# Where row-half matmuls, token-block outputs and attention heads stand in a fused gated block: a Trainium2 kernel re-ordered

## The chip, the cores and the metric

The kernel runs on one core of one Trainium2 chip. The metric is device time in microseconds (us) of that core. Lower is better. A core has a matrix engine (TensorE, here PE, with its weight loads shown as PEld), VectorE (DVE), ScalarE (ACT), GpSimd (POOL) and SyncE (SP, which here issues most DMAs). Each engine works through its own instructions in order; they wait for each other on semaphores. Matmul results land in PSUM, eight banks of 512 floats in each of 128 partitions; all else is in SBUF.

## The reference

```python
g = _sigmoid((x * gate_w).sum(-1, keepdims=True))         # x: 2048 tokens x 640
a = attention(x, wqkv, w_phi, wo)   # 32 heads of 20; feature maps softmax(pq), softmax(-pq)
b = (_silu(x @ w_gate) * (x @ w_up)) @ w_down             # hidden size 1728
return g * a + (1 - g) * b
# attention: kv = sum over tokens of phi_k x v, z = sum of phi_k
#            o = (phi_q @ kv) / (phi_q . z + 1e-6), then @ wo
```

The attention is linear: all keys and values are summed into one small matrix per head before the first query is used. Inputs and output are bf16.

## The kernel before, in words

There are 16 tiles of 128 tokens and four blocks of four tiles. Everything is issued by one list of short words, `ORDER` (lines 40 to 54); each word calls a small function, and what it emits goes to the end of the queues of the engines it uses. So this list alone fixes the order of work on every engine; a tracker (line 57) adds the semaphore waits that the data needs, by ranges of bytes in SBUF and by whole banks in PSUM. The words used below:

- `K`, `S`, `P`, `E`, `V`: keys, their softmax, and the sum over tokens, up to `N` (line 790). These words, the loads and the first stretch of the list are as before in the changed kernel.
- `Q` t (line 619): the query projection of tile t, ten matmuls of 320 columns, and on ACT two exponentials of it into `eq`, a ring of three buffers. `A`, `B`, `C` t (lines 626 to 648) on DVE: the sums, the product with z, and the scale of that tile; `c` t (line 650): the scaling on POOL into `ph`, and a DMA transpose on SP into `phiT`, which has room for two blocks.
- `O` b.part (line 660): a third of the head outputs of block b, matmuls with 64 columns of weights, two side by side in the two column halves of the array; part 2 also has two of 80 rows by 40 columns. ACT copies the result to `oT` and a small rest to `ol`. `o` b (line 688): four DMAs on SP that put the rest into four rows of each half of `oT`: for each half of the block's columns two, the second of which writes the same byte range as the first and so waits until it has landed.
- `F` b.k (line 697): for block b, hidden chunk k of 128, five matmuls of 512 columns for the gate and five for the up projection; ACT takes a tanh of the gate and a copy of the other, DVE and POOL multiply them into `hT`, which has two buffers (block b uses b modulo 2). The last chunk, k = 13, has only 64 hidden values; it is folded so that two tiles lie in rows 0 to 63 and 64 to 127.
- `W` b.p (line 746): the down projection of that last chunk for two tiles of block b, as row-half matmuls: 64 rows by 128 columns, one tile in the upper and one in the lower half of the array, side by side. It opens the accumulation in two pairs of PSUM banks and holds them. Line 756 interleaves the two tiles' matmuls.
- `D` b.u (line 758): for tile u of block b the other 13 chunks of the down projection and five matmuls per half with `wo`, in all 36 of 320 columns, onto what `W` opened; then ACT scales the sum out of PSUM and SP stores it.

PSUM is handed out as four pairs of banks, the least recently used first (lines 453 to 462), without the held ones. The last tile, 15, uses three column parts (320, 224 and 96 columns) in two pairs, so that its stores can begin early.

`W` is called twice in each block, eight times in all; on PE seven of them stand just ahead of a `D`, and one (`W2.0`) ahead of an `F`. The three `O` parts of a block follow each other on PE, which makes four runs of `O`. `F2` words have six extra ACT waits, on a value long reached, ahead of their tanh (line 723).

Of the kernel before, what the change touches and what calls it, by code (L numbers as in the profile page):

```python
# [1 line left out]

# [1 line left out]

# [4 lines left out]
P = 128  # L9
S_TOK = 2048  # L10
D = 640
# [4 lines left out]
NB = 4  # L16
# [25 lines left out]
U0.3 U1.3 U2.3 U0.4 U1.4 U2.4 V3 Y F0.1 M1 i3 M0 F0.0 M2 V4 M3 M4 K0 K1 I S0 V6 V5 S1 P0 K3 K2 P1 E0  # L42
V9 K4 E1 S3 V7 P3 K5 S2 V8 V10 S4 P2 P4 E2 R0 E3 K6 S5 P5 S6 i4 E4 V14 K7 K8 P6 V15 S7 R2 E5 K9 S8
P7 R1 E6 K10 S9 V12 P8 E7 P9 K11 S10 P10 F0.2 R3 F1.2 E8 E9 K12 E10 S11 S12 K14 S14 V11 K13 P11 P12
E11 K15 P14 R4 S13 P13 F1.9 S15 P15 E12 V13 T F1.8 E13 F1.11 E14 Q1 E15 Q0 Q2 N Z A1 A0 J A2 F0.7
F0.9 F1.4 B0 F1.12 B1 F0.4 L C0 F1.7 c0 F1.10 C1 F0.5 B2 c1 F0.11 Q3 C2 F1.0 F0.8 c2 F0.10 B3 Q4
F1.6 A3 C3 Q5 c3 F1.3 F0.13 F0.12 A4 F0.3 B4 F1.5 F0.6 O0.2 O0.1 O0.0 o0 C4 F1.1 F1.13 B5 A5 C5 Q6
c4 Q7 c5 Q8 W0.0 B7 A6 B6 C6 A7 c6 D0.1 D0.0 Q9 C7 W0.1 B8 A8 D0.2 C8 c7 Q10 D0.3 F2.10 F2.9 F2.2 c8
O1.2 A9 O1.1 B9 O1.0 B10 F2.8 o1 C9 Q11 c9 F2.5 F2.11 F2.4 Q12 B11 F2.3 A10 C10 B12 F2.7 A11 C11
W1.1 D1.3 D1.2 A12 c11 c10 Q14 W1.0 D1.0 A14 C12 D1.1 Q13 F3.2 F3.3 c12 O2.2 O2.1 B13 B14 O2.0 o2  # L50
F2.13 A13 F3.12 F3.5 F2.1 C14 Q15 F3.4 F3.9 F2.12 C13 F2.0 A15 c13 F2.6 c14 B15 F3.1 F3.0 F3.6 C15
c15 F3.13 W2.0 F3.7 D2.1 D2.0 F3.11 O3.2 O3.0 O3.1 F3.8 o3 F3.10 W2.1 D2.3 W3.0 D3.0 D3.1 D2.2 W3.1
D3.2 D3.3
"""


# [143 lines left out]
def _build(nc, A_x, A_wqkv, A_w_phi, A_wo, B_x, B_w_gate, B_w_up, B_w_down, gate_w, out):  # L200
# [5 lines left out]
    def sb(name, shape, dtype):  # L206
        t = nc.alloc_sbuf_tensor(name, list(shape), dtype)
        tr.reg(t, "sbuf", nc.lookup_mloc(t).addr)
        return t
# [9 lines left out]
    ident = sb("ident", [P, P], BF16)  # L219
    us = sb("us", [P, 3, 512], BF16)  # L220
    osb = sb("osb", [P, 4, D], BF16)
    ol = sb("ol", [P, 256], BF16)
    kvsb = sb("kvsb", [P, NCH, 64], BF16)
    hmask = sb("hmask", [P, 3], F32)
    zt = sb("zt", [P, NCH, 3], F32)
# [16 lines left out]
    qd = sb("qd", [P, 2, 32], F32)  # L242
    qc = sb("qc", [P, 2, 66], F32)
    hT = sb("hT", [P, 2, 14, 512], BF16)

    wdbase = nc.lookup_mloc(wd).addr
    v1x = nc.alloc_sbuf_tensor_at("v1x", [P, NT - NV, 33 * 21], BF16, offset=wdbase)
    tr.reg(v1x, "sbuf", wdbase)

    def vbuf(t):  # L250
        return v1r[:, t, :] if t < NV else v1x[:, t - NV, :]
# [28 lines left out]
    def bank(b, c0, c1, r0=0, r1=P):  # L280
        return ps[r0:r1, b * 512 + c0:b * 512 + c1]
# [62 lines left out]
    def memset(e, a, v):  # L344
        eo = tr.eng[e]
        return run(e, lambda: eo.memset(a, v), [], [a])
# [67 lines left out]
    def fills(i):  # L414
        if i < 2:
            v1v = (v1r, v1x)[i][:, :, :].rearrange("p b (h d) -> p b h d", d=DH + 1)
            memset("pool", v1v[:, :, H, :], 0.0)
            memset("pool", v1v[:, :, :, DH:DH + 1], 1.0)
        elif i == 2:
            memset("pool", ekr[:, :, 1280:FK], 0.0)  # L420
            memset("pool", krec[:, :, :], 0.0)
        elif i == 3:
            memset("pool", kvsb[:, :, :], 0.0)
            memset("pool", eq[:, :, 1280:FP], 0.0)
            memset("pool", qc[:, :, :], 0.0)
            memset("pool", hmask[:, :], 1.0)
            select(hmask[:, :], [[-40, 3]], ALU.is_ge, 0.0, 0, 1)
            select(hmask[:, :], [[40, 3]], ALU.is_gt, 0.0, 40, -1)
        else:
            memset("pool", ph[:, :, :], 0.0)  # L430
            memset("pool", zh[:, NCH:P], 0.0)
# [225 lines left out]
           ALU.mult)  # L657
        dma("sp", phiT[:, (t // 4) % 2, t % 4, :, :], ph[:, b, :], transpose=True)

    def oitem(bt, part):  # L660
        buf = bt % 2
        pr = next_pair()
        pairs = []
        ms = [2 * part, 2 * part + 1]
        for i, m in enumerate(ms):
            for s in range(2):
                j = 2 * m + s
                if j >= NCH:
                    continue
                if j == NCH - 1:  # L670
                    for g, p0 in enumerate((0, 64)):
                        pairs.append((bank(2 * pr + i, 256 * g, 256 * g + 256, p0, p0 + 40),
                                      kvsb[0:80, j, 0:40], phiT[0:80, buf, 2 * g:2 * g + 2, j, :],
                                      True, True, False))
                    continue
                else:
                    l, o = kvsb[0:120, j, :], bank(2 * pr + i, 0, 512, 64 * s, 64 * s + 64)
                    r = phiT[0:120, buf, :, j, :]
                pairs.append((o, l, r, True, True, False))
        mm(pairs)  # L680
        if part < 2:
            copy("act", oT[:, buf, 2 * part:2 * part + 2, :], halves(pr, 512))
        else:
            copy("act", oT[:, buf, 4, :], bank(2 * pr, 0, 512))
            copy("act", ol[0:40, :], bank(2 * pr + 1, 0, 256, 0, 40))
            copy("act", ol[64:104, :], bank(2 * pr + 1, 256, 512, 64, 104))

    def omove(bt):
        for g in range(2):
            for s in range(2):  # L690
                dma("sp", oT[64 * s + 60:64 * s + 64, bt % 2, :, 256 * g:256 * g + 256],
                    ol[64 * g + 20 * s:64 * g + 20 * s + 20, :])


    nus = [0]

    def fitem(bt, k):
        buf = bt % 2
        pr = next_pair()
        xr = [xT[:, 4 * bt:4 * bt + 4, c, :] for c in range(5)]  # L700
        u = us[:, nus[0] % 3, :]
        nus[0] += 1
        if k < 13:
            g, up = bank(2 * pr, 0, 512), bank(2 * pr + 1, 0, 512)
            h = hT[:, buf, k, :]
            mm(group(g, [(wg[:, c, P * k:P * k + P], xr[c]) for c in range(5)]))
            mm(group(up, [(wu[:, c, P * k:P * k + P], xr[c]) for c in range(5)]))
        else:
            pairs = []
            for b in range(2):  # L710
                pairs += group(bank(2 * pr + b, 0, 256),
                               [(wt[:, c, P * b:P * b + P], xT[:, 4 * bt + b:4 * bt + 4:2, c, :]) for c in range(5)])
            mm(pairs)
            for b in range(2):
                r0, r1 = 64 * b, 64 - 64 * b
                h, g = hT[r0:r0 + 64, buf, k, 0:256], bank(2 * pr + b, 0, 256, r0, r0 + 64)
                actop(h, g, ACTF.Tanh, 0.5)
                actop(u[r0:r0 + 64, 0:256], bank(2 * pr + b, 0, 256, r1, r1 + 64), ACTF.Copy)
                stt(h, h, 1.0, g, ALU.add, ALU.mult)
            h = hT[:, buf, k, 0:256]  # L720
            tt("pool", h, h, u[:, 0:256], ALU.mult)
            return
        if bt == 2:
            for _ in range(NWAIT):
                act.wait_ge(tr.sem["pe"], 1)
        actop(h, g, ACTF.Tanh, 0.5)
        actop(u, up, ACTF.Copy)
        stt(h, h, 1.0, g, ALU.add, ALU.mult)
        tt("pool", h, h, u, ALU.mult)
# [8 lines left out]

    def parts(t):

        pr = dpr[t]
        if t < NT - 1:
            return [(2 * pr[0], 0, 320), (2 * pr[0] + 1, 320, D)]
        return [(2 * pr[0], 0, 320), (2 * pr[0] + 1, 320, 544), (2 * pr[1], 544, D)]

    def hitem(bt, p):

        todo = []
        for b in range(2):
            t = 4 * bt + 2 * p + b  # L750
            dpr[t] = [next_pair() for _ in range(1 + (t == NT - 1))]
            held.update(dpr[t])
            r = slice(64 * b, 64 * b + 64)
            todo.append([(bank(k, 0, c1 - c0), hT[r, bt % 2, 13, P * p:P * p + P], wd[r, 13, c0:c1], True, False, False)
                         for k, c0, c1 in parts(t)])
        mm([m for ab in zip_longest(*todo) for m in ab if m])

    def ditem(bt, u):
        buf = bt % 2
        t = 4 * bt + u  # L760
        tok = slice(P * u, P * u + P)
        ls = [(hT[:, buf, k, tok], wd[:, k, :]) for k in range(13)]
        ls += [(oT[:, buf, m, tok], wog[:, m, :]) for m in range(5)]
        n = len(ls)
        cols = [[(bank(k, 0, c1 - c0), l, r[:, c0:c1], False, i == n - 1, False) for i, (l, r) in enumerate(ls)]
                for k, c0, c1 in parts(t)]
        held.difference_update(used(r) for r in dpr[t])
        o = osb[:, t % 4, :]
        if t < NT - 1:
            mm([p for ab in zip(*cols) for p in ab])  # L770
            actop(o.rearrange("p (b c) -> p b c", b=2), halves(dpr[t][0]), ACTF.Copy, omg[:, t:t + 1])
            stores_done()
            out_evs.append(dma("sp", out2[t * P:(t + 1) * P, :], o))
            return
        for (b, c0, c1), e, ms in zip(parts(t), ("sp", "sp", "act"), cols):
            mm(ms)
            if e == "act":
                run("dve", lambda: dve.tensor_scalar(o[:, c0:c1], bank(b, 0, c1 - c0), omg[:, t:t + 1], None,  # L778
# [11 lines left out]
    def kv_end():  # L790
# [9 lines left out]
        "f": lambda i: load_ffn(FCUT[i], FCUT[i + 1]), "L": load_late_weights, "T": tail_weights, "J": gates,  # L800
        "Y": w_blocks, "I": kv_begin, "N": kv_end, "Z": z_row,
        "Q": qtile, "A": qsum, "B": qden, "C": qscale, "c": qmul,
        "F": fitem, "O": oitem, "o": omove, "W": hitem, "D": ditem,
    }
    for w in LOADS.split() + ORDER.split():
        ops[w[0]](*[int(a) for a in w[1:].split(".") if a])
# [45 lines left out]
```

## Time and profile before

| | us |
|---|---|
| median of 3 runs | 287.82 |
| lowest, highest | 287.75, 288.12 |
| the profiled execution | 289.13 |
| its span, from the first to the last instruction | 287.84 |
| PE busy in it | 283.5 |
| DVE, POOL, ACT busy | 169.8, 156.9, 152.9 |
| granted TensorE clock | 1.0 |

The profiled execution takes 289.13 us; 287.84 of that is the span that its rows cover, 1.29 lie around it. A timeline row gives the start, the time from the first start to the last end, the engine, the line, the operation, what it writes and reads, the shape of the weights (rows*columns), the shape of the moving operand, and how many instructions were merged. A matmul's own duration overlaps the next one's; what counts on PE is the step from one start to the next.

### The profile page before, as it was taken

The page shows a single profiled execution, that of the slowest core. Times are in us where ns is not written, and L with a number is a line of the kernel's source. Part 1 is how long each engine was busy: PE and PEld are TensorE (multiplying, and loading weights), DVE is VectorE, ACT ScalarE, POOL GpSimd, SP SyncE. Part 2 cuts the span into 40 slices and gives each one's busy share as a digit, 9 for nine tenths or more (in the row PEclk, how much of TensorE's full clock was granted, in tenths as well). Part 3 has the DMA queues.
Part 4 walks back from the last instruction along what each step waited for, and adds up shares of the span by engine and source line. Part 5 has one row for each costly group of instructions (what it writes and reads, how often), then busy time and mean ns, then how long its engine had stood idle before and what let it go on. Part 6 is the DMA issues. An engine that isn't in the chain of part 4 may idle for free.

```text
span 287.8 us, 5041 instructions
## 1 busy us (share of the span) xinstructions
PE 283.5 (98%) x1999; PEld 173.5 (60%) x1999; DVE 169.8 (59%) x247; ACT 152.9 (53%) x264; POOL 156.9 (55%) x125
## 2 busy tenths in 40 slices
PE   7899999999999999999999999999999999999997
PEld 6567777675644555456675445767544457556766
DVE  2145757577479998769992787952566983010000
ACT  0668768766665557684434865132786543541112
POOL 8154899979635778947170757260465696130000
DMA  7985789000037264202243022051020053000101
GB/s 232 160 115 120 118 220 363 9 0 3 0 109 248 69 133 76 50 4 50 57 120 73 2 56 52 25 110 38 23 53 4 3 101 73 25 4 26 46 23 48
DMA packets 49374, 21.87 MB, mean 76 GB/s; under 512 B 39462, under 2 KB 49214, under 8 KB 49350
## 3 DMA queue, kind: packets, MB, share of 16 engines
q1 hardware_dynamic: 47830, 20.67, 31.5%
q10 hardware_dynamic: 1520, 0.87, 1.0%
q8 instruction: 16, 0.26, 0.4%
q14 instruction: 8, 0.07, 0.1%
HBM read 9.38 MB, written 2.62 MB: 42 GB/s over the span
## 4 chain that ended last, share of the span: by engine, by line
PE 96%; DMA 2%; ACTq 0%; DVE 0%; issue 0%
PE ps L300 96%; DMA xs<-in_A_x_dram 2%; ACTq L354 0%; PE ps L312 0%; DVE osb L778 0%
## 5 line engine op out<-in xcount | busy, mean ns | idle before, releaser
L328 POOL TENSOR_TENSOR hT<-hT,us 128x512 bf16<-128x512 bf16 (+1 forms) x56 | 66.2, 1193 | 68.4 <-ACT us L318 35.2
L332 DVE SCALAR_TENSOR_TENSOR hT<-hT,ps 128x512 bf16<-128x512 bf16 (+1 forms) x60 | 38.2, 648 | 50.8 <-ACT hT L318 45.0
L300 PE MATMUL ps<-xT,wg 128*128 128x512 bf16 x260 | 64.6, 379 | 0.0
L300 PE MATMUL ps<-xT,wu 128*128 128x512 bf16 x260 | 64.6, 379 | 0.0
L300 PE MATMUL ps<-wd,hT 128*128 128x320 bf16 (+3 forms) x462 | 62.6, 295 | 0.0
L300 PEld LDWEIGHTS ps<-wd,hT 128*128 128x128 bf16 (+1 forms) x462 | 41.8, 98 | 19.2 <-issue 3.1
L328 POOL TENSOR_TENSOR ph<-eq,qc 128x1320 bf16<-128x1320 bf16 x16 | 40.4, 2530 | 15.8 <-DVE qc L645 15.8
L300 PE MATMUL ps<-wqk,xT 128*128 128x320 bf16 x320 | 47.7, 299 | 0.0
L318 ACT ACTIVATE hT<-ps 128x512 bf16<-128x512 f32 (+1 forms) x60 | 34.0, 567 | 20.4 <-PE ps L300 15.2
L300 PEld LDWEIGHTS ps<-xT,wu 128*128 128x128 bf16 x260 | 25.5, 98 | 30.7
L318 ACT ACTIVATE us<-ps 128x512 bf16<-128x512 f32 (+1 forms) x60 | 34.1, 569 | 18.1 <-PE ps L300 17.2
L328 POOL TENSOR_TENSOR ekr<-ekr,krec 128x1280 bf16<-128x1280 bf16 x16 | 37.4, 2360 | 8.2 <-DVE krec L342 8.2
L300 PEld LDWEIGHTS ps<-xT,wg 128*128 128x128 bf16 x260 | 24.9, 98 | 27.7 <-ACT oT L318 1.2
L318 ACT ACTIVATE osb<-ps,omg 128x640 bf16<-128x640 f32 (+2 forms) x17 | 12.9, 758 | 53.0 <-PE ps L300 53.0
L300 PEld LDWEIGHTS ps<-wqk,xT 128*128 128x128 bf16 x320 | 30.6, 98 | 12.4
L318 ACT ACTIVATE eq<-ps 128x640 bf16<-128x640 f32 x32 | 22.5, 704 | 18.5 <-POOL ph L328 8.5
L339 DVE TENSOR_REDUCE ksum<-ekr 128x64 f32<-128x1280 bf16 x16 | 23.5, 1470 | 11.6 <-ACT ekr L318 11.6
L318 ACT ACTIVATE ekr<-ps 128x640 bf16<-128x640 f32 x32 | 22.3, 704 | 8.6 <-PE ps L300 8.1
L339 DVE TENSOR_REDUCE qz<-eq 128x64 f32<-128x1280 bf16 x16 | 23.6, 1478 | 3.6 <-ACT eq L318 3.6
L300 PE MATMUL ps<-wvg,xT 128*128 128x320 bf16 (+1 forms) x160 | 24.1, 300 | 1.2 <-DMA wvg<-in_A_wqkv_dram 1.1
L300 PE MATMUL ps<-wog,oT 128*128 128x320 bf16 (+2 forms) x165 | 24.7, 295 | 0.0
L339 DVE TENSOR_REDUCE qw<-ez 128x64 f32<-128x1280 bf16 x16 | 23.6, 1478 | 0.0
(73 smaller groups left out, 196.6 us busy)
## 6 DMA issues: line engine op xcount, KB each, us to landing
out_dram<-osb SPq DMA_DIRECT2D x15, 160.0 KB, 1.8
wd<-in_B_w_down_dram SPq DMA_DIRECT2D x1, 2080.0 KB, 10.4
wg<-in_B_w_gate_dram SPq DMA_DIRECT2D x1, 1040.0 KB, 10.0
wu<-in_B_w_up_dram SPq DMA_DIRECT2D x1, 1040.0 KB, 12.1
wg<-in_B_w_gate_dram SPq DMA_DIRECT2D x1, 800.0 KB, 6.1
wu<-in_B_w_up_dram SPq DMA_DIRECT2D x1, 800.0 KB, 7.6
wog<-in_A_wo_dram SPq DMA_DIRECT2D x2, 375.0 KB, 4.2
xs<-in_A_x_dram ACTq DMA_DIRECT2D x3, 160.0 KB, 3.9
```

What stands on the lines that cost most here:

```text
L300: last = pe.matmul(o, lhsT=l, rhs=r, start=st, stop=sp_, skip_group_check=sk)
L318: return run("act", lambda: act.activation(o, i, func, scale=scale), rd, [o])
L328: return run(e, lambda: eo.tensor_tensor(o, a, b, op), [a, b], [o])
L332: return run("dve", lambda: dve.scalar_tensor_tensor(out=o, in0=a, scalar=s, in1=b, op0=op0, op1=op1), rd, [o])
L339: return run("dve", lambda: dve.tensor_reduce(o, i, AX.X, ALU.add), [i], [o])
```

## The change

1. `W` b is one word per block. `D` b.0 and `D` b.1 now come first and open their own accumulation; `W` b then adds the row-half matmuls of tiles 0 and 1 onto it (and their results leave), and in the same breath opens tiles 2 and 3, which `D` b.2 and `D` b.3 close. For the very last tile only two column parts (320 and 224) are opened so; the third, 96 columns, takes the 64 hidden values from `hz`, a buffer of 128 rows whose upper half is zeroed at the start and whose lower half DVE fills, and is one group of 19 matmuls of 128 rows.
2. The third block (number 2 in the code) keeps its FFN values in `hx`, which lies over the value tiles `v1r` and the weights `wvg`, both no longer needed after the keys. So `F2` words no longer wait for `D0`, and stand as early as right after `N`.
3. `O` takes a first and a last block: `O0.1`, `O1.2` and `O2.4`. The parts go in the order 0, 1, 2, and `O2.4` does both last blocks in one run of six parts, in which ACT copies one bank and DVE the other. The DMAs of `omove` follow inside the same word; `ol` has a buffer for each of two blocks.
4. A `D` is given to PE as two groups, 26 matmuls of hidden chunks and 10 with `oT`, so that only the second waits for `oT`.
5. The list is a new one from `N` on.

```diff
+E11 K15 P14 R4 S13 P13 F1.9 S15 P15 E12 V13 T F1.8 E13 F1.11 E14 Q1 E15 Q0 Q2 N A1 A0 F2.12 Z F1.3 J
+F0.3 F0.13 B0 F0.12 F0.6 B1 C1 F0.10 L F2.5 F0.11 F0.9 C0 A2 c0 F0.4 F1.4 B2 F2.6 c1 F2.11 Q3 C2
+F0.8 c2 A3 F2.10 B3 F2.9 Q5 C3 F1.7 F1.1 F0.7 Q4 B5 A4 c3 F1.13 A5 F1.5 B4 F2.2 F2.3 F1.12 C4 F2.1
+Q6 F1.10 A6 c4 F1.0 F0.5 C5 O0.1 B6 Q7 A7 c5 C6 Q8 c6 F1.6 B8 D0.1 B7 A8 Q9 D0.0 C7 C8 B9 c7 W0 c8
+D0.2 F2.8 A9 C9 Q11 Q10 D0.3 B10 O1.2 c9 A10 C10 Q12 B12 B11 c10 F2.7 A11 Q13 A12 F2.13 A13 C11 B13
+C12 c11 D1.0 C13 D1.1 W1 D1.2 c12 Q14 c13 Q15 A15 D1.3 F3.10 B15 C15 F2.4 F3.12 F3.1 c15 F3.3 B14
+F3.11 A14 F3.0 C14 c14 F3.4 F2.0 F3.2 F3.6 F3.7 F3.5 O2.4 F3.9 F3.8 D2.1 F3.13 D2.0 W2 D2.2 D2.3
+D3.0 D3.1 W3 D3.2 D3.3
...
+    hx = [nc.alloc_sbuf_tensor_at("hx%d" % i, [P, n, 512], BF16, offset=nc.lookup_mloc(a).addr)
+          for i, (a, n) in enumerate(((v1r, 8), (wvg, 6)))]
...
+            memset("pool", hz[:, :], 0.0)
...
+        e = "dve" if two else "act"
+        if part < 2 and not two:
+            copy("act", oT[:, buf, 2 * part:2 * part + 2, :], halves(pr, 512))
+            return
+        copy("act", oT[:, buf, 2 * part, :], bank(2 * pr, 0, 512))
         if part < 2:
+            copy(e, oT[:, buf, 2 * part + 1, :], bank(2 * pr + 1, 0, 512))
         else:
+            copy(e, ol[0:40, buf, :], bank(2 * pr + 1, 0, 256, 0, 40))
+            copy(e, ol[64:104, buf, :], bank(2 * pr + 1, 256, 512, 64, 104))
...
+    def orun(b0, b1):
+        for part in range(3):
+            for b in range(b0, b1):
+                oitem(b, part, b1 - b0 > 1)
+        for b in range(b0, b1):
+            omove(b)
...
+    def hitem(bt):
+        for p in range(2):
+            todo = []
+            for b in range(2):
+                t = 4 * bt + 2 * p + b
+                if p:
+                    d_open(t)
+                r = slice(64 * b, 64 * b + 64)
+                todo.append([(bank(k, 0, c1 - c0), hbuf(bt, 13)[r, P * p:P * p + P], wd[r, 13, c0:c1], p == 1, p == 0, False)
+                             for k, c0, c1 in parts(t)])
+            mm([m for ab in zip(*todo) for m in ab])
+        for t in (4 * bt, 4 * bt + 1):
+            held.remove(used(dpr[t]))
+            d_out(t)
+        if bt == NB - 1:
+            copy("dve", hz[64:P, :], hbuf(bt, 13)[64:P, P:2 * P])
...
+        if u < 2:
+            d_open(t)
...
+            mm(both[:26])
+            mm(both[26:])
+            if u > 1:
+                held.remove(used(dpr[t]))
+                d_out(t)
...
+        ps3 = parts(t) + [(2 * next_pair(), 544, D)]
+        cols.append(group(bank(ps3[2][0], 0, D - 544), [(l, r[:, 544:D]) for l, r in [(hz[:, :], wd[:, 13, :])] + ls]))
```

More of the change, by code (lines that the diff above doesn't have):

```diff
@@ L1 @@
 from __future__ import annotations
-from itertools import zip_longest
 import concourse.bass as bass
@@ L44 @@
 P7 R1 E6 K10 S9 V12 P8 E7 P9 K11 S10 P10 F0.2 R3 F1.2 E8 E9 K12 E10 S11 S12 K14 S14 V11 K13 P11 P12
[L45 to L53, printed above, removed]
+E11 K15 P14 R4 S13 P13 F1.9 S15 P15 E12 V13 T F1.8 E13 F1.11 E14 Q1 E15 Q0 Q2 N A1 A0 F2.12 Z F1.3 J
[6 more added lines that the diff above has]
+D3.0 D3.1 W3 D3.2 D3.3
 """
@@ L221, in _build @@
     osb = sb("osb", [P, 4, D], BF16)
-    ol = sb("ol", [P, 256], BF16)
+    ol = sb("ol", [P, 2, 256], BF16)
     kvsb = sb("kvsb", [P, NCH, 64], BF16)
@@ L244, in _build @@
     hT = sb("hT", [P, 2, 14, 512], BF16)
+    hz = sb("hz", [P, P], BF16)
     wdbase = nc.lookup_mloc(wd).addr
@@ L248, in _build, with hbuf @@
     tr.reg(v1x, "sbuf", wdbase)
+    hx = [nc.alloc_sbuf_tensor_at("hx%d" % i, [P, n, 512], BF16, offset=nc.lookup_mloc(a).addr)
+          for i, (a, n) in enumerate(((v1r, 8), (wvg, 6)))]
+    for x, a in zip(hx, (v1r, wvg)):
+        tr.reg(x, "sbuf", nc.lookup_mloc(a).addr)
+    def hbuf(bt, k):
+        if bt == 2:
+            return hx[k // 8][:, k % 8, :]
+        return hT[:, bt % 2, k, :]
     def vbuf(t):
@@ L658, in qmul, with oitem @@
         dma("sp", phiT[:, (t // 4) % 2, t % 4, :, :], ph[:, b, :], transpose=True)
-    def oitem(bt, part):
+    def oitem(bt, part, two):
         buf = bt % 2
@@ L680, in oitem @@
         mm(pairs)
+        e = "dve" if two else "act"
[3 more added lines that the diff above has]
+        copy("act", oT[:, buf, 2 * part, :], bank(2 * pr, 0, 512))
         if part < 2:
-            copy("act", oT[:, buf, 2 * part:2 * part + 2, :], halves(pr, 512))
+            copy(e, oT[:, buf, 2 * part + 1, :], bank(2 * pr + 1, 0, 512))
         else:
-            copy("act", oT[:, buf, 4, :], bank(2 * pr, 0, 512))
-            copy("act", ol[0:40, :], bank(2 * pr + 1, 0, 256, 0, 40))
-            copy("act", ol[64:104, :], bank(2 * pr + 1, 256, 512, 64, 104))
+            copy(e, ol[0:40, buf, :], bank(2 * pr + 1, 0, 256, 0, 40))
+            copy(e, ol[64:104, buf, :], bank(2 * pr + 1, 256, 512, 64, 104))
     def omove(bt):
@@ L691, in omove @@
                 dma("sp", oT[64 * s + 60:64 * s + 64, bt % 2, :, 256 * g:256 * g + 256],
-                    ol[64 * g + 20 * s:64 * g + 20 * s + 20, :])
+                    ol[64 * g + 20 * s:64 * g + 20 * s + 20, bt % 2, :])
+    def orun(b0, b1):
[4 more added lines that the diff above has]
+            omove(b)
     nus = [0]
     def fitem(bt, k):
-        buf = bt % 2
         pr = next_pair()
@@ L704, in fitem @@
             g, up = bank(2 * pr, 0, 512), bank(2 * pr + 1, 0, 512)
-            h = hT[:, buf, k, :]
+            h = hbuf(bt, k)
             mm(group(g, [(wg[:, c, P * k:P * k + P], xr[c]) for c in range(5)]))
@@ L715, in fitem @@
                 r0, r1 = 64 * b, 64 - 64 * b
-                h, g = hT[r0:r0 + 64, buf, k, 0:256], bank(2 * pr + b, 0, 256, r0, r0 + 64)
+                h, g = hbuf(bt, k)[r0:r0 + 64, 0:256], bank(2 * pr + b, 0, 256, r0, r0 + 64)
                 actop(h, g, ACTF.Tanh, 0.5)
@@ L719, in fitem @@
                 stt(h, h, 1.0, g, ALU.add, ALU.mult)
-            h = hT[:, buf, k, 0:256]
+            h = hbuf(bt, k)[:, 0:256]
             tt("pool", h, h, u[:, 0:256], ALU.mult)
@@ L739, in parts, with d_open, d_out @@
     def parts(t):
[L741 to L756, printed above, removed]
+        k = 2 * dpr[t]
+        return [(k, 0, 320), (k + 1, 320, D if t < NT - 1 else 544)]
+    def d_open(t):
+        dpr[t] = next_pair()
+        held.add(dpr[t])
+    def hitem(bt):
[14 more added lines that the diff above has]
+            copy("dve", hz[64:P, :], hbuf(bt, 13)[64:P, P:2 * P])
+    def d_out(t):
+        o = osb[:, t % 4, :]
+        actop(o.rearrange("p (b c) -> p b c", b=2), halves(dpr[t]), ACTF.Copy, omg[:, t:t + 1])
+        stores_done()
+        out_evs.append(dma("sp", out2[t * P:(t + 1) * P, :], o))
     def ditem(bt, u):
@@ L761, in ditem @@
         tok = slice(P * u, P * u + P)
-        ls = [(hT[:, buf, k, tok], wd[:, k, :]) for k in range(13)]
+        ls = [(hbuf(bt, k)[:, tok], wd[:, k, :]) for k in range(13)]
         ls += [(oT[:, buf, m, tok], wog[:, m, :]) for m in range(5)]
         n = len(ls)
-        cols = [[(bank(k, 0, c1 - c0), l, r[:, c0:c1], False, i == n - 1, False) for i, (l, r) in enumerate(ls)]
-                for k, c0, c1 in parts(t)]
-        held.difference_update(used(r) for r in dpr[t])
-        o = osb[:, t % 4, :]
[L769 to L775, printed above, removed]
+        if u < 2:
+            d_open(t)
+        cols = [[(bank(k, 0, c1 - c0), l, r[:, c0:c1], u < 2 and i == 0, u > 1 and i == n - 1, False)
+                 for i, (l, r) in enumerate(ls)] for k, c0, c1 in parts(t)]
+        if t < NT - 1:
+            both = [p for ab in zip(*cols) for p in ab]
+            mm(both[:26])
[3 more added lines that the diff above has]
+                d_out(t)
+            return
+        o = osb[:, t % 4, :]
+        held.remove(used(dpr[t]))
+        ps3 = parts(t) + [(2 * next_pair(), 544, D)]
+        cols.append(group(bank(ps3[2][0], 0, D - 544), [(l, r[:, 544:D]) for l, r in [(hz[:, :], wd[:, 13, :])] + ls]))
+        for (b, c0, c1), e, ms in zip(ps3, ("sp", "sp", "act"), cols):
             mm(ms)
@@ L802, in _build @@
         "Q": qtile, "A": qsum, "B": qden, "C": qscale, "c": qmul,
-        "F": fitem, "O": oitem, "o": omove, "W": hitem, "D": ditem,
+        "F": fitem, "O": orun, "W": hitem, "D": ditem,
     }
```

## The prediction, as it was made before the changed kernel was run

> **What bounds the kernel now.** I read the page first: busy times and the chain that ended last.
>
> ```profile
> span 287.8 us, 5041 instructions
> PE 283.5 (98%) x1999; PEld 173.5 (60%) x1999; DVE 169.8 (59%) x247; ACT 152.9 (53%) x264; POOL 156.9 (55%) x125
> PE 96%; DMA 2%; ACTq 0%; DVE 0%; issue 0%
> ```
>
> PE carries 96% of the chain, and the rest is the start. So only two things can move the time: PE's own steps, and new waits of PE. The table of waits has no PE wait after the first 10 us. The change keeps the number of matmuls, so next I looked in PE's timeline for places where the step from one matmul to the next is longer than its columns need.
>
> The plain steps: a `D` of 36 matmuls of 320 columns runs from 136.89 to 141.78 below, 4.89 / 36 = 0.1358 us each. Nine `F` groups (78.75 to 98.18, 90 matmuls of 512) give 0.2159 each.
>
> ```profile
> 121.69 1.24 PE L300 MATMUL ps<-xT,wu 128*128 128x512 bf16 x5
> 122.86 1.38 PE L300 MATMUL ps<-phiT,kvsb 120*64 120x512 bf16 x12
> 124.18 1.25 PE L300 MATMUL ps<-xT,wg 128*128 128x512 bf16 x5
> ...
> 127.44 4.24 PE L300 MATMUL ps<-wqk,xT 128*128 128x320 bf16 x30
> 131.61 4.08 PE L300 MATMUL ps<-wd,hT 64*128 64x320 bf16 x30
> 135.53 1.52 PE L300 MATMUL ps<-wog,oT 128*128 128x320 bf16 x10
> 136.89 3.69 PE L300 MATMUL ps<-wd,hT 128*128 128x320 bf16 x26
> 140.42 1.52 PE L300 MATMUL ps<-wog,oT 128*128 128x320 bf16 x10
> 141.78 1.52 PE L300 MATMUL ps<-wqk,xT 128*128 128x320 bf16 x10
> ```
>
> The reader is to see `W0.0` inside the row at 131.61. The 30 query matmuls ahead should be done at 127.44 + 30 x 0.1358 = 131.514, so the first row-half matmul starts 0.096 late. From 131.61 to 136.89 are 5.28; less 36 plain steps, 4.89, the four row-half matmuls and the way out of them take 0.39. Two pairs side by side need 2 x 0.136 = 0.27, so 0.12 is lost behind them.
>
> ```profile
> 131.61 0.11 PEld L300 LDWEIGHTS ps<-wd,hT 64*128 64x128 bf16 x4 [0.26 <-issue]
> 131.98 3.37 PEld L300 LDWEIGHTS ps<-wd,hT 128*128 128x128 bf16 x26 [0.27 <-issue]
> ```
>
> The weight loads say the same: the next shape's weights are not loaded while the old one works. PEld idles 0.26 and 0.27 on both sides, with nobody to wait for. All eight `W` have it: starts of `W` to the word behind the `D` are 5.27 or 5.28 (178.42 to 183.69, 190.04 to 195.32, 260.38 to 265.65, 275.53 to 280.81). The predecessor doesn't matter. So one `W` costs 0.096 + 0.39 = **0.486**.
>
> The `O` run has it too. The five matmuls of 121.69 are done at 121.69 + 1.079 = 122.769; the run starts at 122.86, 0.09 late. Its 12 matmuls in 6 pairs need 5 x 0.216 + 0.11 (the short pair: half of 512 columns) = 1.19, and took 124.18 - 122.86 = 1.32: 0.13 more.
>
> **The change part by part.** One `W` per block: the two pairs of the removed group don't vanish, they join the other group at 0.136 a pair, or 0.145 at most (that allows 0.10 instead of 0.12 for the exit; `O`'s excess of 0.13 with its own inner change of shape lies on both sides). Each block saves 0.486 - 2 x 0.145 = 0.195, four blocks **0.78**. The weight loads of the group take 0.11 for four, so eight are no bound.
>
> Four runs of `O` become three. The removed run's entry is 0.09; of its 0.13 I take 0.11 for the exit, since the inner change to 40 columns remains: **0.20**.
>
> The last tile's third part was a fifth row-half matmul beside another (`W3.1` took 5.28 like the rest, so it was free); now it is a 19th step of 96 columns. PE's last rows give 13 such steps from 284.98 to 285.53, 0.042 each: **+0.04**. Sum so far: -0.94.
>
> A rule of the Trainium skill bears on this (TensorEngine Tiling (Array Packing), section Key Properties): a change of tiling mode drains the array, a change of tile within a mode doesn't. The rows agree, with 0.09 to 0.12 a change. With the warm fixed part of one matmul's latency on the page TensorE: Matmul & The Clock Gate (section Single matmul latency: 398 cycles at 2.4 GHz, 0.166 us) as the price, the ten changes that go would be an estimated 1.66 us; the rows decide against it.
>
> What costs nothing, and what hides it. The memset of `hz` (POOL memsets there are 0.20 to 0.69) stands ahead of an idle time of POOL of 5.5 us before its first key scaling at 25.28. The copy into `hz` stands 4.9 us (`D3.2`) before its reader. The six ACT waits of each `F2` lengthen tanh's start by 0.08 (156.12 is 0.28 behind its matmuls, elsewhere it is 0.20); ACT has 38 us of work for 66 us of PE between `N` and `O0.1`. `Z` comes 2.2 us later on PE and so z lands later, but its first reader `B0` now stands three `F` words later. `W`'s two stores stand on SP behind the ring's `c7` and ahead of `c8`, whose tile is read 70 us later.
>
> New waits are the other half. In front of each I count the words.
>
> *`O2.4`.* Six parts go through four pairs, so the fifth, the sixth and `F3.9` take a pair of this run. With T the end of `F3.5`: part i's matmuls end at T + 0.09 + 0.432 i, copying starts 0.2 behind (as tanh does behind its matmuls). DVE has no row of a copy of 512 columns from PSUM. The nearest:
>
> ```profile
> L332 DVE SCALAR_TENSOR_TENSOR hT<-hT,ps 128x512 bf16<-128x512 bf16 x52 | 35.0, 684 | 45.2 <-ACT hT L318 45.0
> L324 DVE CAST wqk<-ps 128x640 bf16<-128x640 f32 x2 | 1.6, 824 | 2.2 <-PE ps L300 2.2
> ```
>
> The first has the same elements (successive ones start 0.60 apart), the second the same kind with 640: 824 x 512 / 640 = 0.66. At 0.684 the third copy ends at T + 0.72 + 2 x 0.60 + 0.68 = T + 2.60; `F3.9` may start at T + 0.09 + 4 x 0.432 + 2 x 0.35 + 0.1 = T + 2.62. That is a wait of 0 to 0.1 (a semaphore has to travel). At 0.824 a copy and 0.74 apart it is 0.41. I take 0.05, by the row with the same elements. Bounds: 0 and 0.41. It can't gain anything: without it, PE is simply in step.
>
> *Head rests for `D0.1`.* The four DMAs of `omove`:
>
> ```profile
> 124.74 1.94 ACT L318 ACTIVATE oT<-ps 128x1024 bf16<-128x1024 f32 x2
> 126.71 5.48 SPq L354 DMA_DIRECT2D oT<-ol  x4
> ```
>
> Four issues of 0.62 to 0.79 make 2.7 of the 5.48; the rest is two waits of 1.4 for the landing. So a rest lands 2.1 behind its issue, two of the same half 4.3, all four 6.9. ACT is done 126.68 - 124.18 = 2.5 after the run's end E. `D0.1` reads columns 128 to 255, that is the first half: E + 2.5 + 4.3 = E + 6.8. It reads `oT` after `Q7`, `Q8`, `F1.6` (1.36 + 1.36 + 2.16) and its own 26 matmuls (3.53): E + 8.4. Slack 1.6. `D1.0` has 9.5 of PE behind its E and its rests there at 2.8 + 4.3 = 7.1 (ACT first empties `D0.3`); `D2.1` has 7.9, its `ol` from DVE at 1.4, so 5.7. Slack over 2 in both.
>
> *All four pairs at `W0`.* `D0.1` and `D0.0` hold two, `W0` needs the others, the last of them `Q9`'s. Its exponentials wait for `c6` (three buffers), that for `C5` (3.3, to E + 2.3), `B6`, `A7` and `C6` (3.3): with `B6` at the 2.95 that the trace has for such an instruction beside POOL, E + 5.3, 6.8, 10.1; `c6` 2.5 and ACT 1.43 give E + 14.0. PE comes to `W0` after 16.0. Slack 2.
>
> The same skill page warns that row tiling presses on PSUM, since row tiles write to different banks (section Gotcha 1: PSUM Pressure); no row of this trace shows eight banks asked for at once, so only the slack above stands for it.
>
> *The other engines as a whole:* between `N` and `O0.1` DVE has 7 `A` (1.4), 6 `B` (1.3), 6 `C` (3.35) and 29 `F` (0.6) = 56 us for 66 of PE (before, to `O0.2`: 39 for 44); from there to `O1.2` 25 for 31, to `O2.4` 44 for 57. No stretch is tighter than one that PE got through unhindered.
>
> So -0.94 + 0.05 = -0.89: the profiled execution's 289.13 would be 288.24 (span 286.95), the median, 1.31 below that execution, **286.9**.
>
> **The rivals.** (1) *The run of heads binds:* DVE copies at 0.82, or stretched beside POOL, as the z product is: 0.82 alone, 2.95 at 135.47. For it: POOL has a product of 1.2 in each `F`. Against it: the 52 rows with an operand in PSUM average 0.684 with hardly any spread. Price 0.41 to 1.1: 287.3 to 288.0.
>
> (2) *The pairs at `W0`, or another queue that the sums miss:* a slip of 1 to 2 us beyond the slack, 287.3 to 288.2. For it: contention of DVE and POOL is common in this trace. Against it: the slacks.
>
> (3) *Slower, by the head rests:* if a `D` waits for all four DMAs, they land at E + 2.5 + 6.9 = 9.4 and PE stalls 1.0 in `D0.1`, and by the same count 0.2 and 0.4 in `D1.0` (9.7 for 9.5) and `D2.1` (8.3 for 7.9): 286.9 + 1.6 = 288.5. With the first two alone it decides from the point where they land 2.5 us later than I count (1.6 slack, then 0.9 of gain). For it: each of the DMAs is one wait behind another on SP. Against it: the tracker goes by byte ranges, and before, `D0.1` started at 131.99, ahead of the last landing (132.19 + 1.4).
>
> (4) *It doesn't do what it says:* the row-half pairs of a longer group run one after the other: four more pairs of 0.136 per block, 2.2 in all, slower as well (289.1). The four loads in 0.11 and the 0.39 speak against it.
>
> **How the numbers follow.** Forecast 0.72 (286.6 to 287.2: the 0.41 and a gain of 1.2 are its ends), (1) 0.11, (2) 0.07, (3) 0.07, (4) 0.03. The range from 286.6 to 287.7 takes in the forecast and most of (1). 0.2%, about what a measurement here can tell from no change, is 0.58 us: faster means below 287.24. Faster 0.73, same 0.14, slower 0.13.
>
> **What would show it.** PE's timeline: four rows of row-half matmuls, eight in each, with PEld idle 0.26 before and behind; three `O` runs, the last with 24 matmuls. No PE wait after 10 us but perhaps one at `F3.9`, released by DVE `oT`. DVE copies of 128x512 near 0.68. In a `D` no gap between `hT` and `oT`. The prediction is wrong if PE waits anywhere for `oT` or at a `W`, or if a group's entry and exit grow with its length.

## The result, and the profile after

| | before | changed |
|---|---|---|
| median, with the number of runs on the same chip | 287.91 (6) | 286.63 (6) |
| ratio, 95% interval | | 0.996 (0.9949 to 0.9972) |
| the profiled execution | 289.13 | 286.57 |
| its span | 287.84 | 285.32 |

The forecast was 286.9 in a range from 286.6 to 287.7, so this median lies just inside the lower end. A second measurement of the changed kernel (further down) gave 287.0 against 287.75. The first lines of the page after:

```profile
span 285.3 us, 5052 instructions
PE 282.6 (99%) x1999; PEld 174.7 (61%) x1999; DVE 172.9 (61%) x256; ACT 150.0 (53%) x260; POOL 158.0 (55%) x126
PE 99%; DVE 0%; issue 0%
```

PE is still the bound and runs as many matmuls as before. Next is PE's timeline after, around the first `W`, and then its weight loads there. The first columns are start and length, the last one the number of instructions merged.

```profile
155.72 3.69 PE L308 MATMUL ps<-wd,hT 128*128 128x320 bf16 x26
159.25 1.52 PE L308 MATMUL ps<-wog,oT 128*128 128x320 bf16 x10
160.71 4.36 PE L308 MATMUL ps<-wd,hT 64*128 64x320 bf16 x34
164.90 1.52 PE L308 MATMUL ps<-wog,oT 128*128 128x320 bf16 x10
```

```profile
160.70 0.39 PEld L308 LDWEIGHTS ps<-wd,hT 64*128 64x128 bf16 x8 [0.26 <-issue]
161.35 3.38 PEld L308 LDWEIGHTS ps<-wd,hT 128*128 128x128 bf16 x26 [0.26 <-issue]
```

Eight row-half loads now stand in one piece, with PEld idle 0.26 ahead and 0.26 behind, once per block instead of twice. From the first of the ten `oT` matmuls (159.25) to the `oT` matmuls of `D0.2` (164.90) are 5.65. Ten and 26 plain steps of 0.1358 are 4.89, so the group of four tiles costs 0.76. A group of two tiles cost 0.486.

**Where to measure.** The span fell by 2.5, the median by 1.3 and, the second time, by 0.75. In the profiled executions the kernel's start makes the difference. Two marks leave it out: the row of the last key sum, and the end of the last matmul. The first fence is before, the second after.

```profile
75.64 0.51 PE L300 MATMUL ps<-v1x,ekr 128*128 128x63 bf16 x11
...
285.53 0.38 PE L300 MATMUL ps<-wog,oT 128*128 128x96 bf16 x5
```

```profile
74.17 0.51 PE L308 MATMUL ps<-v1x,ekr 128*128 128x63 bf16 x11
...
283.02 0.38 PE L308 MATMUL ps<-wog,oT 128*128 128x96 bf16 x5
```

By these rows the stretch is 210.27 before (285.53 + 0.38 - 75.64) and 209.23 after: 1.04 less. Below I take it from the start of the last single key-sum matmul, to the nanosecond, and call it **the stretch**: 209.959 before and 208.912 after, so **-1.05**. Behind it, up to the span's end, lie 1.92 to 1.93 in both. The other 1.47 were gone at the first of these rows already.

### The profile page after: what moved, and what is told of

Its sections match the earlier page's. It is cut to its first block, busy times and chain, and to the rows that moved or that the text cites. A ratio compares the mean times of both kernels' runs of the same rounds, so it can differ in the third digit from the quotient of the medians.

```text
span 285.3 us, 5052 instructions
## 1 busy us (share of the span) xinstructions
PE 282.6 (99%) x1999; PEld 174.7 (61%) x1999; DVE 172.9 (61%) x256; ACT 150.0 (53%) x260; POOL 158.0 (55%) x126
## 4 chain that ended last, share of the span: by engine, by line
PE 99%; DVE 0%; issue 0%
PE ps L308 97%; PE ps L494 1%; PE ps L320 1%; DVE osb L819 0%
## 5 line engine op out<-in xcount | busy, mean ns | idle before, releaser
L336 POOL TENSOR_TENSOR hT<-hT,us 128x512 bf16<-128x512 bf16 (+1 forms) x42 | 50.8, 1217 | 37.1 <-DVE hT L340 21.6
L340 DVE SCALAR_TENSOR_TENSOR hT<-hT,ps 128x512 bf16<-128x512 bf16 (+1 forms) x45 | 28.9, 649 | 37.5 <-ACT hT L326 26.8
L308 PE MATMUL ps<-wd,hT 128*128 128x320 bf16 (+3 forms) x349 | 46.7, 294 | 0.0
L308 PEld LDWEIGHTS ps<-wd,hT 128*128 128x128 bf16 (+1 forms) x349 | 31.8, 98 | 13.1 <-issue 1.6
L326 ACT ACTIVATE hT<-ps 128x512 bf16<-128x512 f32 (+1 forms) x45 | 25.5, 567 | 21.3 <-PE ps L308 18.9
L336 POOL TENSOR_TENSOR hx<-hx,us 128x512 bf16<-128x512 bf16 (+1 forms) x14 | 16.1, 1158 | 16.4 <-DVE hx L340 11.0
```

Source lines behind the costliest of these rows:

```text
L308: last = pe.matmul(o, lhsT=l, rhs=r, start=st, stop=sp_, skip_group_check=sk)
L326: return run("act", lambda: act.activation(o, i, func, scale=scale), rd, [o])
L336: return run(e, lambda: eo.tensor_tensor(o, a, b, op), [a, b], [o])
L340: return run("dve", lambda: dve.scalar_tensor_tensor(out=o, in0=a, scalar=s, in1=b, op0=op0, op1=op1), rd, [o])
```

## The experiments

Each run is read by its stretch, against 208.91 of the changed kernel and 209.96 of before. The median stands beside it. Differences are to the changed kernel's code except where the text says otherwise.

### The profiles again

The change had moved the first profile's start as well. To see what is spread, I took the changed kernel again and both kernels in further single profiles, with no edit.

> The changed kernel once more, unchanged, for the time against the kernel before: the stretch from the last matmul of the key sums to the end 208.91 again; the time 0.9 to 1.3 below the kernel before. What exceeds 1.05 is put down to the DMAs at the start: theory, the profiled start differs from run to run (first F at 12.70 before, 11.32 changed) and this one may differ from both; rival, the changed kernel's start is always earlier, near 11.3.

> The kernel before once more, for its start. Theory (the first 12 us are the DMAs of the first loads, which land earlier or later from run to run in either kernel): the first F begins anywhere from 11.0 to 12.7, and the stretch from the last key-sum matmul to the end is 209.96 again. Rival (the kernel before starts late by itself, as in its first profile): the first F at 12.5 or later again.

> The same a second time: theory 11.0 to 12.7 and 209.96; rival 12.5 or later.

> The changed kernel a third time. Theory: the first F between 11.0 and 12.7, the stretch 208.91. Rival (the changed kernel always starts early): 11.2 to 11.4 again.

Measured: the changed kernel's median was 287.0 (12 runs) against 287.75, ratio 0.9974 (0.9963 to 0.9984). The gain of 0.75 is below the 0.9 to 1.3 expected; 1.05 of 287.8 would be a ratio of 0.9964, which both intervals contain. Its stretch was 208.907 in both further profiles; before's was 209.958 in both. So the stretch repeats to 0.005. The start does not. PE's timeline there, of before in its first profile, of before in the first repeat, and of the changed kernel in its repeat:

```profile
5.02 0.99 PE L300 MATMUL ps<-wvg,xT 128*128 128x320 bf16 x6
...
7.96 0.99 PE L300 MATMUL ps<-wvg,xT 128*128 128x320 bf16 x6 [1.12 <-DMA wvg<-in_A_wqkv_dram]
...
12.70 1.24 PE L300 MATMUL ps<-xT,wg 128*128 128x512 bf16 x5
```

```profile
5.13 1.78 PE L300 MATMUL ps<-wvg,xT 128*128 128x320 bf16 x6
...
11.94 1.24 PE L300 MATMUL ps<-xT,wg 128*128 128x512 bf16 x5
```

```profile
5.20 0.99 PE L308 MATMUL ps<-wvg,xT 128*128 128x320 bf16 x6
...
11.22 1.24 PE L308 MATMUL ps<-xT,wg 128*128 128x512 bf16 x5
```

The first `F` starts at 12.70, 11.94 and 11.84 in before's three profiles, at 11.32, 11.22 and 11.44 in the changed kernel's. So the rival for before, a first `F` at 12.5 or later again, falls. Mainly two things move it: whether a load is awaited (1.12 in the first fence), and how fast the six value matmuls at about 5 us go (0.99 or 1.78). The other kernels below have their first `F` at 11.09 to 11.97. Among them `e4_act_alone` and `e5_one_wait`, which up to there are the changed kernel's code, start at 11.97 and 11.91 with the slow matmuls, so the changed kernel doesn't always start early, and that rival falls as well. From the first `F` to the last key sum it is 63.17 in every profile but before's first (63.25). So 1.05 of the 2.5 us belongs to the change. Whether before starts later more often, three profiles of it don't settle.

### `W` in two groups again, and in four

If the price is that of a change of shape, two groups per block give back four times one price, and four groups twelve times; if the new list or the waits made the gain, neither does. In `e1_two_groups` the pairs of tiles 0 and 1 go between the two groups of the `D` ahead of `W`; in `e2_four_groups` there are four groups of one pair each, two plain matmuls apart (its values stand behind the `#`).

```diff
+BEFORE_W = {(0, 0), (1, 1), (2, 0), (3, 1)}
+HEARLY = [[(0, 0), (0, 1)]]           # e2: [[(0, 0)], [(0, 1)], [(1, 0)]]
+HLAST = [(1, 0), (1, 1)]              # e2: [(1, 1)]
...
-            mm(both[26:])
+            rest = both[26:]
+            if (bt, u) in BEFORE_W:
...
+                for pcs in HEARLY:
+                    mm([m for p, c in pcs for m in hpair(bt, p, c, t)])
+                    mm(rest[:2])
+                    rest = rest[2:]
+            mm(rest)
```

> The changed kernel, but each block's row-half matmuls in two groups again: the pairs of tiles 0 and 1 go between the two groups of the D ahead of W, ten plain matmuls apart from the rest; the list of words, the buffers and the heads stay. Measured from the last matmul of the key sums to the end of the last matmul (209.96 before, 208.91 changed), so that the start's DMAs don't enter. Theory (a price on each entry into and exit from row halves, 0.216 us a group by the changed trace): four more groups, 208.91 + 0.86 = 209.77; in the time +0.9 against the changed kernel. Rival (the gain comes from the new list, that is from waits and not from the changes of shape): stays at 208.9.

> The changed kernel, with the four row-half pairs of a block in four groups of one pair, two plain matmuls between the groups. Theory (a fixed price per group, whatever its length): twelve more groups than in the changed kernel at 0.19 to 0.22, 208.91 + 2.3 to 2.6 = 211.2 to 211.5. Rival (the price grows with the length of the group or with what is behind it, so that short groups are cheap): under 210.5.

Measured: two groups 209.759 (median 287.43, ratio to before 0.9986, 0.9977 to 0.9996); four groups 211.462 (289.21, ratio 1.0045, 1.003 to 1.006). The weight loads of the first of the two:

```profile
159.12 0.12 PEld L313 LDWEIGHTS ps<-wd,hT 64*128 64x128 bf16 x4 [0.26 <-issue]
159.50 1.20 PEld L313 LDWEIGHTS ps<-wog,oT 128*128 128x128 bf16 x10 [0.26 <-issue]
160.96 0.11 PEld L313 LDWEIGHTS ps<-wd,hT 64*128 64x128 bf16 x4 [0.26 <-issue]
161.34 3.37 PEld L313 LDWEIGHTS ps<-wd,hT 128*128 128x128 bf16 x26 [0.26 <-issue]
```

The 0.26 are there four times instead of twice. By the stretch, four added groups cost 0.85 and twelve 2.55: **0.213 a group** in both, whether it holds one pair, two or four. In the single starts of the changed kernel's trace a group of four pairs reads: in 0.231 instead of 0.136, the next step 0.147, two steps at 0.136, out 0.228, the next step 0.147. So it is 0.095 in, 0.092 out, twice 0.01 for the step behind, and 0.004 by which the second of two matmuls side by side starts later. The pairs themselves cost a plain step each. The rival, that the list or the waits made this gain, falls: the list is the same here, and PE's waits behind the start are none in either run.

### The first part alone, in the old list

`e6_old_list` starts from before: one `W` per block (with the third part of the last tile as a plain group), `D` in two groups, the old order with `W`, `D` and a few neighbours moved as this needs, the third block's values where they were, four runs of heads. The fence shows only the stretches of the list that differ, cut out of longer lines.

```diff
-c4 Q7 c5 Q8 W0.0 B7 A6 B6 C6 A7 c6 D0.1 D0.0 Q9 C7 W0.1 B8 A8 D0.2 C8 c7 Q10 D0.3
+c4 Q7 c5 Q8 B7 A6 B6 C6 A7 c6 D0.1 D0.0 C7 W0 B8 D0.2 Q9 A8 C8 c7 Q10 D0.3
...
-W1.1 D1.3 D1.2 A12 c11 c10 Q14 W1.0 D1.0 A14 C12 D1.1 Q13
+D1.0 D1.1 A12 c11 c10 W1 D1.2 Q14 A14 C12 D1.3 Q13
...
-F3.13 W2.0 F3.7 D2.1 D2.0 F3.11 O3.2 O3.0 O3.1 F3.8 o3 F3.10 W2.1 D2.3 W3.0 D3.0 D3.1 D2.2 W3.1 D3.2 D3.3
+F3.13 F3.7 D2.1 D2.0 W2 D2.3 F3.11 F3.8 F3.10 O3.2 O3.0 O3.1 o3 D2.2 D3.0 D3.1 W3 D3.2 D3.3
```

> The kernel before with the first part of the change alone: one row-half group per block and D in two groups, in the old list with D, W and a few neighbours moved (the last F words now stand ahead of the fourth block's heads); heads in four runs, FFN values of the third block in the old buffer. Theory: 209.96 - 4 x 0.216 = 209.1, if the two pairs of banks held from D to W make nobody wait. Rival (the change works only with the values' new place and the new list): PE waits at W or at the heads, and the stretch stays at 209.9 or more.

Measured: 209.234, or -0.72 (median 286.94, ratio 0.9965, 0.9953 to 0.9978). That is four groups of 0.213, less about 0.04 for the third part and a wait of 0.08 that I had not foreseen. While `D2.2`'s pair of banks is held, three are left, and the third part of the last `O` gets the one that `F3.10` had; ACT copies out of it until 257.86. The part's first matmul starts at 258.00, 0.272 instead of 0.216 behind the pair before, and the last matmul of the run 0.029 instead of 0.004 behind its partner.

So the `W` gain needs neither the new place of the values nor the new list. The 0.32 by which the changed kernel is ahead are the removed run of heads (0.229, next section) and this wait. That the long run needs the new place and the new list is how the change was built; no run tried it without them. The intervals of the medians can't tell this kernel from the changed one; the stretch can, by 0.32.

### The last two blocks' heads in two runs

```diff
-F3.6 F3.7 F3.5 O2.4 F3.9 F3.8
+F3.6 F3.7 O2.3 F3.5 F3.9 O3.4 F3.8
```

> The changed kernel, with the heads of the last two blocks in two runs, two F words apart, copied by ACT alone. Theory (entry 0.093, first pair 0.021, exit 0.095 for a run, no wait of PE in either form): 208.91 + 0.21 = 209.12. Rival (the long run hides a wait for its banks, so that two runs cost less): 208.9 to 209.0. Rival (ACT alone is late for the F behind): 209.3 or more, with PE idle there.

Measured: 209.136, so one run costs **0.229** (median 287.0, ratio 0.997, 0.9956 to 0.9985). The starts give 0.093 in, 0.021 behind the first pair, 0.098 out, 0.01 behind that, and twice 0.003 by which the second matmul of a pair starts later. The 0.021 stands behind the first pair of every run, also where the 80 x 40 pair doesn't follow it; at the change to 40 columns nothing is lost.

### One engine for the copies in the long run

```diff
-                oitem(b, part, b1 - b0 > 1)
+                oitem(b, part, False)
```

> The changed kernel, with the six parts of the last two blocks' heads copied by ACT alone. Theory (six parts in four pairs; ACT takes 0.92 a part from 235.26 on): the sixth part waits some 0.55 for the second part's pair, the F behind some 0.5 for the third's: 208.91 + 1.1 = 210.0. Rival (the copying engine doesn't matter, because PE has slack in that run): 208.9.

Measured: 209.975, or +1.07 (median 288.1, ratio 1.001, 1.0 to 1.0021). First PE's timeline around `O2.4` in the changed kernel, then DVE's, then PE's in this one:

```profile
234.59 2.58 PE L308 MATMUL ps<-phiT,kvsb 120*64 120x512 bf16 x24
237.10 1.25 PE L308 MATMUL ps<-xT,wg 128*128 128x512 bf16 x5
```

```profile
235.26 2.48 DVE L332 CAST oT<-ps 128x512 bf16<-128x512 f32 x4 [0.32 <-PE ps L308]
237.66 1.78 DVE L332 CAST ol<-ps 40x256 bf16<-40x256 f32 x4
```

```profile
237.90 0.52 PE L308 MATMUL ps<-phiT,kvsb 120*64 120x512 bf16 x4 [0.40 <-ACT oT L326]
238.82 1.25 PE L308 MATMUL ps<-xT,wg 128*128 128x512 bf16 x5 [0.40 <-ACT oT L326]
```

With two engines PE passes through the run with no wait. With one it waits ahead of the sixth part and ahead of `F3.9`; by the starts it loses 0.56 and 0.47 there, somewhat more than the idle time shown. ACT's 1024-element copies release both. The long run is worth 0.229, and with one engine the kernel is 1.07 slower, so 0.84 slower than with two runs: the long run pays only with the copies shared.

### A `D` in one piece

If `D` waits for the heads' rests ahead of its first matmul, the 26 matmuls no longer run while the DMAs are under way, and the wait measures when the rests land, and how many of the four DMAs are awaited.

```diff
-            mm(both[:26])
-            mm(both[26:])
+            mm(both)
```

> The changed kernel, with each D as one group of 36 matmuls, so that its first matmul waits for the head rows too. By the changed trace the first two of the four DMAs land at 151.3, 184.05 and 242.6, and the D words that read them begin at 149.47, 183.41 and 241.43. Theory (two of the four DMAs are waited for): +1.9, +0.65 and +1.2, 208.91 + 3.7 = 212.6. Rival (all four are waited for): they land some 2.7 later, +4.6, +3.3 and +3.9, about 220. Rival (the split is needless): 208.9.

Measured: 213.012, or +4.10 (median 290.9, ratio 1.0111, 1.0092 to 1.013). PE loses 2.01 ahead of `D0.1`, 0.785 ahead of `D1.0` and 1.31 ahead of `D2.1`. SP's issues of the four DMAs, then PE at `D0.1`:

```profile
147.64 5.48 SPq L362 DMA_DIRECT2D oT<-ol  x4
```

```profile
148.99 1.24 PE L308 MATMUL ps<-xT,wu 128*128 128x512 bf16 x5
152.08 3.69 PE L308 MATMUL ps<-wd,hT 128*128 128x320 bf16 x26 [1.85 <-ACT eq L326]
```

SP issues the four at 147.64, 149.80, 150.50 and 152.50. PE resumes at 152.08, before the fourth is issued: it waits for the first two only, and resumes 2.27 behind the start of the second issue. At `D1.0` and `D2.1` it is 2.12 and 2.13; the expectation had 2.0 at all three, so its sum was 0.4 too low. The row names an ACT write of `eq` as the releaser. `D` doesn't read `eq`, and in the changed kernel `D0.1` starts at 149.47, ahead of that write's end at 151.39; so the name is wrong here. For the other two waits the profile names the DMA. In the changed kernel the second issue is at 149.27, so by the same 2.27 `oT` is ready at 151.55, and the `oT` matmuls of `D0.1` start at 153.00: the slack is 1.45.

### Full rows instead of row halves

If it is the shape that costs, matmuls of 128 rows have no such price, but can't lie side by side. Here the 64 rows of weights lie twice in SBUF, each copy beside 64 rows of zeros, and `W` is eight plain matmuls (seven of 320 columns and one of 224 in the last block).

```diff
-                r = slice(64 * b, 64 * b + 64)
-                todo.append([(bank(k, 0, c1 - c0), hbuf(bt, 13)[r, P * p:P * p + P], wd[r, 13, c0:c1], p == 1, p == 0, False)
+                todo.append([(bank(k, 0, c1 - c0), hbuf(bt, 13)[:, P * p:P * p + P], wz[b][:, c0:c1], p == 1, p == 0, False)
```

> The changed kernel without row halves: the 64 hidden values' weights lie twice, each time with 64 rows of zeros, and W is eight plain matmuls of 128 rows. Theory: no change of shape at W, but 8 x 0.136 = 1.09 instead of 0.754 per block, 208.91 + 4 x 0.33 = 210.2; so a row-half group of four tiles beats full rows, and one of two tiles (0.486 for two, 0.97 per block) beat it by little. Rival (the entry and exit belong to W's place or its waits, not to its shape): they stay, 8 x 0.136 + 0.2, and the stretch is 211.

Measured: 210.197, or +1.29 (median 288.12, ratio 1.0016, 1.0005 to 1.0027). PE's timeline at the same `W`:

```profile
160.96 0.30 PE L311 MATMUL ps<-wd,hT 128*128 128x320 bf16 x1
...
161.91 0.30 PE L311 MATMUL ps<-wz,hT 128*128 128x320 bf16 x1
162.05 3.69 PE L311 MATMUL ps<-wd,hT 128*128 128x320 bf16 x26
```

From 160.96 to 162.05 are 1.09, eight plain steps with nothing lost on either side, against 0.755 for the row halves. So the price belongs to the shape. Row halves still win: a pair saves one step of 0.136, and worked out from these, two pairs already pay for the 0.213 (0.485 against 0.543), and one pair doesn't (0.349 against 0.272).

By the stretch none of these kernels beats the changed one.

## Why the prediction was right, and where it was not

- **The bound and the place of the gain** held. All of the -1.05 adds up from PE's steps: 4 x 0.213 + 0.229 - 0.04 = 1.04. PE's only wait in the changed profile is 0.8 at its very start. The forecast had 0.89; the 0.16 between are 0.07 from `W`, 0.03 from the heads and a wait of 0.05 that didn't come, all on one side.
- **`W`: too small by a tenth.** The step that gave 0.195 a block charged each pair that joins a group 0.145, the upper of two values. `W2.0`, ahead of an `F`, has none of the 5.27 or 5.28 that the working gives for all eight, but by its starts it cost the same. The joining pairs cost a plain 0.136; the 0.01 stands once behind the entry and once behind the exit, whatever the length. With 0.136, the working's other end, the sum would have been 0.214, and 0.213 was measured.
- **The removed run of heads: 0.229 instead of 0.20.** The entry of 0.09 held. The step "0.11 for the exit, since the inner change to 40 columns remains" failed: the inner change costs nothing, and the missing 0.02 follows the first pair of each run, so it goes with the run.
- **The third part** cost about 0.04, as counted.
- **The wait at `F3.9`: none, where 0.05 was taken.** The durations held: DVE's copies took 0.692, 0.681, 0.681 and 0.679 and started 0.60 apart, as the row with the same elements said and not the scaled 0.824, and the third ended at 237.15, 0.03 to 0.05 from the forecast. What failed is the step that let `F3.9` wait for it. By the code, `F3.9`'s first five matmuls, at 237.10, write the bank that ACT empties, and ACT's third copy ended at 236.83; the bank that DVE empties is written by the next five, at 238.19, with 1.04 to spare. Had `F3.9` needed DVE's bank first, it would have started some 0.1 later. The tighter place was the sixth part, which the working didn't time. By the code it waits for both copies of the second part; DVE's ended at 236.55 and the part started at 236.67. In the run with ACT alone PE starts 0.05 behind the copy that it waits for, so the slack here was 0.07. A DVE copy of 0.82, with 0.74 from start to start, would have ended at 236.82 and held up the sixth part by an estimated 0.2, and `F3.9` by nothing of its own; the 0.41 of rival (1) was too dear. All this is read from the traces and the code; no run tried it.
- **Head rests:** slack 1.45 where 1.6 was counted. The rival of all four DMAs falls by the experiment of `D` in one piece.
- **The pairs at `W0`:** `Q9`'s exponentials ended at 157.36 and `W0` came at 160.71: slack 3.3 instead of 2.
- **The rival that pairs run one after the other** falls with the 0.755 for four pairs.
- **The profiled execution's own time** was forecast as 288.24 and was 286.57. That step failed: it subtracted the gain from a profile of before whose start was late by a DMA wait of 1.12, and no later profile of before had it. The median, taken 1.31 below that execution, did not suffer: 286.9 against 286.63 and 287.0. That they lie on both sides of it is in part luck: the two medians differ by 0.37, more than the forecast's error of 0.16 by the stretch, so they alone wouldn't have shown which terms were off.

## What to carry to other kernels

On a full matrix engine, look at the step from the last matmul of one shape to the first of the next. Here a change between full weights and row halves, or 64-column weights, cost 0.09 to 0.10 each way, which busy times hide; where the same shows, gather the odd-shaped matmuls into few, longer groups. Before the longer group is made, count who frees its banks: here a second engine for the copies was the difference between 0.23 gained and 0.84 lost (1.07 less 0.23). And measure a change of 1 us between two marks behind the kernel's start; the start alone moved by more (first `F` from 11.09 to 12.70).

## What the runs showed of the hardware that was not expected

- **A change between 128*128 weights and 64*128 or 120*64 costs the same at every place**: 0.09 to 0.10 in, 0.09 to 0.10 out and 0.01 in the step behind each, after matmuls of 512 and of 320 columns, for groups of 2 to 8 row-half matmuls, and for 64*128 as for 120*64 (which adds 0.021 behind its first pair). From 120*64 to 80*40 nothing is lost.
- **The early matmuls are slower in some executions** at a granted clock that reads 1.0: the steps between six value matmuls at about 5 us are 0.24 to 0.27 instead of 0.136 in before's two repeats and in the runs with ACT alone and with `D` in one piece. The six took 0.99 in before's first profile and 1.78 in its first repeat.
- **A DMA of 10 KB inside SBUF releases its waiters late**: SP's next DMA onto the same range started 2.0 to 2.2 behind it in the changed kernel and 2.0 to 2.6 in before, PE 2.12 to 2.27 with `D` in one piece. The releaser that the profile names for such a wait can be an engine that has nothing to do with it.
